# A fused attention and mixer kernel: six token tiles transposed by DMA, the first queries in column parts, and a second queue for loads

## The chip, the cores and the metric

The kernel runs on one core of one Trainium2 chip. The metric is the device time of one execution in microseconds (us), lower is better; three executions of the kernel before gave 1246.11, 1246.24 and 1246.83 us. A core has a matrix engine (TensorE, PE in the profile, with its weight loads shown as PEld), a vector engine (VectorE, DVE), a scalar engine (ScalarE, ACT), GpSimd (POOL) and a sync engine (SyncE, SP) that here only issues transfers. Transfers run on 16 DMA engines; SP and ACT each have a queue that feeds them (SPq and ACTq in the profile).

## The reference

The input `A_x` has 2048 tokens of width 512. It is normalised, and the result feeds two branches whose outputs are multiplied:

```python
xn = _layernorm(x)
# A: 32 heads of width 128, 2048 cached keys and values
q = (xn @ wq).reshape(B, Sq, H, Dh).transpose(0, 2, 1, 3)
p = _softmax(einsum("bhqd,bhkd->bhqk", q, k_cache) * (Dh ** -0.5))
s = einsum("bhqk,bhkd->bhqd", p, v_cache).transpose(0, 2, 1, 3).reshape(B, Sq, H * Dh) @ wo
# B: a mixer and an MLP on xn
h = _gelu(_layernorm(xn) @ w1)
hs = (the four column quarters of h, moved by +1, -1, +2, -2 tokens) @ w2
x1 = xn + hs
g = _silu(x1 + _gelu(_layernorm(x1) @ w3) @ w4)
return x + s * g
```

All arrays are bf16. The attention is by far the largest part.

## The kernel before, in words

A token tile is 128 tokens; there are 16 of them, t = 0 to 15. Every engine runs its own instructions in the order in which the program wrote them (`pin` keeps it), and waits between engines go by semaphores. DMAs take eight semaphores in turn, so each one also waits until the DMA issued eight before it has landed.

The program has a start of some 47 us, which this case is about, then the MLP, and then a long loop over 128 units (a head and 512 queries each) in which TensorE computes scores, ScalarE their exponentials, VectorE the sums, and TensorE the products with the values.

The start runs like this. `load_x` brings a token tile; tiles 0 to 7 are loaded first, tiles 1 and 3 and half of `w1` on ACT's queue and the rest on SP's. Behind them on SP come the four slices of `wq` for heads 0 to 3 (`load_w`), `w2`, and tiles 8 to 15. Eleven matmuls on zeros keep TensorE busy until the first tile is there.

`ln1(t, tr)` is the first normalisation: on VectorE the statistics of tile t + 1, then the normalised tile t into `xall`; the reciprocal root between them is on GpSimd. As the statistics of the next tile stand ahead of the normalisation, a late load of tile t + 1 holds tile t too, and everything behind it on VectorE. Then `tr` transposes the tile into `xnT`, which holds the tokens as columns. `tr_pe` does this with four 128-column matmuls against the identity into the PSUM pool `psO` and a ScalarE copy; `tr_dma` does it with one transposing DMA on SP, which needs neither.

`m1_tile` multiplies one transposed tile with `w1` (16 matmuls of 128 columns), `gelu_tile` applies the activation on ScalarE and writes `hT`; for tokens from 512 on, `m1(c0, 512)` does this for four tiles at once, with 16 matmuls of 512 columns. `m2(t)` multiplies four shifted pieces of `hT` with `w2` (four matmuls of 512 columns), and `x1(t)` adds the result to `xall` on VectorE, which frees the PSUM buffer of `m2(t)`. `q_mm` and `q_copy` make the queries of one unit: four matmuls of 512 columns into one of the two buffers `xa` and `xm` of the pool `psX`, and a copy to SBUF on ScalarE. `q_ahead` does both for a unit ahead of the loop and alternates between the two buffers.

Their order in the program before: tiles 0 to 3 are each transposed by TensorE, with `m1_tile` of tiles 0 to 3 between and behind them; for tiles 4 to 7 (`tr_q`) the queries of units 0 to 3 are made, each ahead of the TensorE transposition of one tile; then `m2` of tiles 0 and 1, `ln1` of tiles 8 to 11 with DMA transpositions, `m1(512, 512)`, `x1` of tiles 0 and 1, the queries of units 4 to 7, `m2` of tiles 2 and 3, `ln1` of tiles 12 to 15 with DMA transpositions, the loads of a further slice of `wq` and of `w3` on SP, `m1(1024, 512)`, and so on.

Of the kernel before, what the change touches and what calls it, by code (L numbers as in the profile page):

```python
# [10 lines left out]
FP32 = mybir.dt.float32  # L11
BF16 = mybir.dt.bfloat16
# [5 lines left out]
def kernel(  # L18
# [15 lines left out]
    nc = tc.nc  # L34
    P = nc.NUM_PARTITIONS

    x2d = A_x.flatten_outer_dims()
    out2d = out.flatten_outer_dims()
    Sq, D = x2d.shape
# [6 lines left out]
    DC = D // P  # L46
# [4 lines left out]
    HG = 4  # L51
# [10 lines left out]
    pin = tc.keep_in_program_order  # L62

    def pool(name, bufs=1, space=None, **kw):
        if space is not None:
            kw["space"] = space
        return tc.tile_pool(name=name, bufs=bufs, **kw)
# [3 lines left out]
    xnT = const.tile([P, DC, Sq], BF16, name="xnT")  # L71
# [19 lines left out]
    psO = ent(pool("psO", 2, PSUM))  # L91
    psX = ent(pool("psX", 1, PSUM))
    mid = ExitStack()
    psS = mid.enter_context(pool("psS", 2, PSUM, reuse_waits="tile"))
# [4 lines left out]
    pL = left.enter_context(pool("pL", reuse_waits="tile"))  # L99
# [4 lines left out]
    w2_v = B_w2.rearrange("(dc p) j -> p dc j", p=P)  # L104
    w3_v = B_w3.rearrange("(dc p) f -> p dc f", p=P)

    def mm(out, lhsT, rhs, start, stop):
        pin(nc.tensor.matmul(out=out, lhsT=lhsT, rhs=rhs, start=start, stop=stop))  # L108
# [7 lines left out]
        out=ident[:], in0=diag[:], scalar1=0.0, scalar2=None, op0=ALU.is_equal))  # L116

    units = [(g, qt, hh) for g in range(NG) for qt in range(QT) for hh in range(HG)]
# [5 lines left out]
    kTs, vBs, wqs, wos, oTs, st = {}, {}, {}, {}, {}, {}  # L124
# [30 lines left out]
    def load_w(h, eng=nc.sync):  # L155
        wqs[h] = wqp.tile([P, DC, Dh], BF16, name="wq_h")
        pin(eng.dma_start(out=wqs[h][:], in_=wq_v[:, :, h * Dh:(h + 1) * Dh]))

    vX = {}
    xin = {}  # L160

    def load_x(t, eng):
        xin[t] = tokp.tile([P, D], BF16, tag="ta", bufs=10, name="xin")
        pin(eng.dma_start(out=xin[t][:], in_=xsrc[t]))

    w1_sb = pL.tile([P, DC, D], BF16, name="w1_sb")
    w2_sb = pL.tile([P, DC, D], BF16, name="w2_sb")
# [22 lines left out]
    def ln1_stats(t):  # L192
        stats(xin[t][:], mv1, rs1, t)

    def ln1_norm(t):
        norm_to(xall[:, t, :], xin.pop(t)[:], mv1, rs1, t)

    def tr_pe(t):
        tp = psO.tile([P, DC, P], FP32, tag="ps_o", name="ps_o")
        for dc in range(DC):  # L200
            mm(tp[:, dc, :], xall[:, t, dc * P:(dc + 1) * P], ident[:], True, True)
        pin(nc.scalar.activation(out=xnT[:, :, t * P:(t + 1) * P], in_=tp[:], func=ACT.Identity))  # L202
# [17 lines left out]
    def m2(t, pl=psO, tag="ps_o"):  # L220
        ps = pl.tile([P, D], FP32, tag=tag, name="ps_o")
        for jc in range(DC):
            c0 = BASE_J[jc] + t * P - SHIFT[jc]
            mm(ps[:], hT[:, jc, c0:c0 + P], w2_sb[:, jc, :], jc == 0, jc == DC - 1)
        return ps
# [41 lines left out]
    def q_mm(u, dcs, tag="xa"):  # L267
        g, qt, hh = units[u]
        if dcs[0] == 0:
            st[u] = dict(psq=psX.tile([P, 512], FP32, tag=tag, name="ps_q"))  # L270
        for dc in dcs:
            mm(st[u]["psq"][:], wqs[g * HG + hh][:, dc, :],
               xnT[:, dc, qt * 512:(qt + 1) * 512], dc == 0, dc == DC - 1)

    def q_copy(u, eng=None):
        qT = qtp.tile([P, 512], BF16, name="qT")
        if eng is None:
            pin(nc.vector.tensor_copy(out=qT[:], in_=st[u].pop("psq")[:]))  # L278
        else:
            pin(nc.scalar.activation(out=qT[:], in_=st[u].pop("psq")[:], func=ACT.Identity))  # L280
        st[u]["qT"] = qT
# [227 lines left out]
    for t, eng in enumerate([nc.sync, nc.scalar, nc.sync]):  # L509
        load_x(t, eng)  # L510
    pin(nc.scalar.dma_start(out=w1_sb[:, 2:4, :], in_=w1_v[:, 2:4, :]))
    pin(nc.sync.dma_start(out=w1_sb[:, 0:2, :], in_=w1_v[:, 0:2, :]))
    load_x(3, nc.scalar)
    pin(nc.scalar.activation(out=junk[:], in_=ones_t[:], func=ACT.Gelu_apprx_tanh))
    for t in range(4, 8):
        load_x(t, nc.sync)
    for h in range(HG):
        load_w(h)
    pin(nc.sync.dma_start(out=w2_sb[:], in_=w2_v))
    wps = psX.tile([P, 512], FP32, tag="xm", name="ps_warm")  # L520

    def warm_mm(n):
# [9 lines left out]
    def ln1(t, tr):  # L532
        if t + 1 < NT:
            ln1_stats(t + 1)
        ln1_norm(t)
        tr(t)

    def m1_tile(t, pl, tag):
        ps = pl.tile([P, DC, P], FP32, tag=tag, name="ps_m1")
        for jc in range(DC):  # L540
            for dc in range(DC):
                mm(ps[:, jc, :], w1_sb[:, dc, jc * P:(jc + 1) * P],
                   xnT[:, dc, t * P:(t + 1) * P], dc == 0, dc == DC - 1)
        return ps

    def gelu_tile(t, ps):
        for jp in range(DC // 2):
            b = BASE_J[2 * jp] + t * P
            pin(nc.scalar.activation(
                out=hT[:, 2 * jp:2 * jp + 2, b:b + P], in_=ps[:, 2 * jp:2 * jp + 2, :],  # L550
                func=ACT.Gelu_apprx_tanh))
# [2 lines left out]
    ln1(0, tr_pe)  # L554
    warm_mm(1)
    ln1(1, tr_pe)
    pm = [m1_tile(0, psX, "xa")]
    ln1(2, tr_pe)
    gelu_tile(0, pm[0])
    pm.append(m1_tile(1, psX, "xm"))  # L560
    ln1(3, tr_pe)
    gelu_tile(1, pm[1])
    for t in (2, 3):
        gelu_tile(t, m1_tile(t, psS, "ps_s"))

    made = []

    def q_ahead(u):
        q_mm(u, range(DC), ("xa", "xm")[len(made) % 2])
        q_copy(u, nc.scalar)  # L570
        made.append(u)

    def tr_q(t):
        q_ahead(t - 4)
        tr_pe(t)

    for t in range(8, 16):
        load_x(t, nc.sync)
    for t in range(4, 8):
        ln1(t, tr_q)  # L580
    pend = [(t, m2(t)) for t in range(2)]
    for t in range(8, 12):
        ln1(t, tr_dma)
    m1(512, 512)
# [1 line left out]
        x1(t, ps)  # L586
    for u in range(HG, 2 * HG):
        q_ahead(u)
    pend = [(t, m2(t)) for t in range(2, 4)]
    for t in range(12, 16):  # L590
        ln1(t, tr_dma)
    wqs[H - 1] = pL.tile([P, DC, Dh], BF16, name="wq_e")
# [131 lines left out]
    for n in range(UB * SPU):  # L724
        u, p = divmod(n, SPU)
# [52 lines left out]
    t0 = 4 * (QT - 1)  # L778
# [144 lines left out]
```

## Time and profile before

| what | value |
|---|---|
| median of three executions | 1246.24 us |
| the profiled execution: its time | 1246.23 us |
| its span, first to last instruction | 1244.5 us |
| TensorE busy | 1231.6 us, 99% of the span |
| ScalarE busy | 1106.5 us, 89% |
| VectorE busy | 1008.4 us, 81% |
| first matmul on a token tile | at 5.87 us |
| first matmul of `m1(512, 512)` | at 17.68 us |
| first matmul of `m1(1024, 512)` | at 26.35 us |

Times in the profile count from the first instruction. The profiled execution's time is 1.7 us more than its span; it stands 0.01 us from the median, so it can be read as a typical one. A matmul's recorded duration (219 ns for 128 columns, 379 ns for 512) is longer than the distance to the next one, because matmuls overlap; the work is counted by the distance between starts, or by the pieces in the chain of work that ended last, which is told on from one instruction to the next.

### The profile page before, as it was taken

The page shows a single profiled execution, that of the slowest core. Times are in us where ns is not written, and L with a number is a line of the kernel's source. Part 1 is how long each engine was busy: PE and PEld are TensorE (multiplying, and loading weights), DVE is VectorE, ACT ScalarE, POOL GpSimd, SP SyncE. Part 2 cuts the span into 40 slices and gives each one's busy share as a digit, 9 for nine tenths or more (in the row PEclk, how much of TensorE's full clock was granted, in tenths as well). Part 3 has the DMA queues.
Part 4 walks back from the last instruction along what each step waited for, and adds up shares of the span by engine and source line. Part 5 has one row for each costly group of instructions (what it writes and reads, how often), then busy time and mean ns, then how long its engine had stood idle before and what let it go on. Part 6 is the DMA issues. An engine that isn't in the chain of part 4 may idle for free.

```text
span 1244.5 us, 16193 instructions
## 1 busy us (share of the span) xinstructions
PE 1231.6 (99%) x5757; PEld 606.7 (49%) x5873; DVE 1008.4 (81%) x1458; ACT 1106.5 (89%) x1112; POOL 27.4 (2%) x77
## 2 busy tenths in 40 slices
PE   9999999999999999999999999999999999999998
PEld 4444444444444444444444444444444444444445
DVE  7712778888888888888888888888888988999996
ACT  5344999999999999999999999999999999999996
POOL 5300000000000000000000000000000000000000
PEclk9999999999999999999999999999999999999999
DMA  6661123453345525553354424644345425553332
GB/s 179 149 135 35 26 44 64 102 103 81 63 80 109 101 48 85 84 117 77 56 102 86 106 55 69 104 101 72 72 86 113 101 59 90 98 111 62 79 77 65
DMA packets 241810, 107.15 MB, mean 86 GB/s; under 512 B 192704, under 2 KB 225472, under 8 KB 241728
## 3 DMA queue, kind: packets, MB, share of 16 engines
q1 hardware_dynamic: 241024, 105.51, 42.9%
q8 instruction: 46, 0.75, 0.3%
q10 hardware_dynamic: 704, 0.59, 0.1%
q14 instruction: 36, 0.29, 0.1%
HBM read 67.50 MB, written 2.36 MB: 56 GB/s over the span
## 4 chain that ended last, share of the span: by engine, by line
PE 98%; issue 1%; DVE 0%; ACT 0%; DMA 0%; POOL 0%; DVEq 0%
PE ps_s L108 41%; PE ps_o L108 38%; PE ps_q L108 8%; PE ps_wo L108 8%; PE ps_m L108 2%; PE ps_oh L108 0%; DMA xin<-in_A_x_dram 0%; ACT qT L280 0%; ACT xnT L202 0%; PE ps_w L108 0%; DVE tm L791 0%; DVE bn L183 0%; DVE y L808 0%; DVE xall L188 0%; DVE y L800 0%
## 5 line engine op out<-in xcount | busy, mean ns | idle before, releaser
L294 ACT ACTIVATE pT<-ps_s 128x1024 bf16<-128x1024 f32 x1016 | 1036.6, 1023 | 60.8 <-PE ps_s L108 7.7
L108 PE MATMUL ps_s<-qT,kT 128*128 128x512 bf16 (+1 forms) x2061 | 608.5, 377 | 5.1
L108 PE MATMUL ps_o<-pT,vb 128*128 128x512 bf16 x1979 | 589.0, 379 | 0.3
L305 DVE TENSOR_TENSOR acc<-acc,pT 128x2048 bf16<-128x2048 bf16 x254 | 307.5, 1211 | 104.5 <-ACT pT L294 104.2
L108 PEld LDWEIGHTS <-kT 128*128 128x128 bf16 x2064 | 234.0, 113 | 217.9
L108 PEld LDWEIGHTS <-vb 128*128 128x128 bf16 x1984 | 193.9, 98 | 216.7
L300 DVE TENSOR_TENSOR acc<-pT 128x2048 bf16<-128x2048 bf16 x127 | 155.2, 1222 | 39.3 <-ACT pT L294 39.1
L108 PE MATMUL ps_q<-xnT,wq_h 128*128 128x512 bf16 x459 | 168.5, 379 | 0.1
L108 PE MATMUL ps_wo<-wo_h,oT 128*128 128x512 bf16 x449 | 168.5, 379 | 0.0
L309 DVE TENSOR_TENSOR acc<-acc 128x1024 bf16<-128x1024 bf16 x127 | 87.9, 692 | 4.3
L366 DVE TENSOR_TENSOR oT<-ps_o,rb 128x512 bf16<-128x512 f32 x127 | 86.5, 681 | 1.3 <-DMA rb<-dr 0.8
L108 PEld LDWEIGHTS <-oT 128*128 128x128 bf16 x513 | 57.6, 113 | 58.5 <-ACT oT L490 0.3
L346 DVE TENSOR_REDUCE sm<-tT 128x4 f32<-128x512 bf16 x124 | 83.7, 675 | 0.3 <-DMA tT<-acc 0.3
L278 DVE CAST qT<-ps_q 128x512 bf16<-128x512 f32 x116 | 79.2, 683 | 0.0
L108 PEld LDWEIGHTS <-wq_h 128*128 128x128 bf16 x508 | 49.5, 98 | 59.1 <-issue 0.3
L430 DVE TENSOR_TENSOR sacc<-ps_wo,sacc 128x512 f32<-128x512 f32 x96 | 65.6, 683 | 0.0
L315 DVE TENSOR_TENSOR acc<-acc 128x512 bf16<-128x512 bf16 x126 | 53.6, 426 | 4.3
L245 ACT ACTIVATE h2T<-ps_s 128x1024 bf16<-128x1024 f32 x28 | 28.6, 1023 | 26.1 <-PE ps_s L108 25.4
L108 PE MATMUL ps_s<-xn2T,w_sb 128*128 128x512 bf16 x220 | 48.6, 379 | 0.2
L108 PEld LDWEIGHTS <-w_sb 128*128 128x128 bf16 x336 | 30.3, 98 | 32.1
L108 PEld LDWEIGHTS <-h2T 128*128 128x128 bf16 x224 | 21.9, 98 | 26.2
L108 PE MATMUL ps_m<-w_sb,h2T 128*128 128x512 bf16 x110 | 33.9, 379 | 0.2
(71 smaller groups left out, 329.1 us busy)
## 6 DMA issues: line engine op xcount, KB each, us to landing
rb<-dr SPq DMA_DIRECT2D x127, 256.0 KB, 4.1
vb<-in_A_v_cache_dram SPq DMA_DIRECT2D x62, 256.0 KB, 3.3
wq_h<-in_A_wq_dram SPq DMA_DIRECT2D x32, 128.0 KB, 3.5
wo_h<-in_A_wo_dram SPq DMA_DIRECT2D x32, 128.0 KB, 3.3
w_sb<-in_B_w_dram SPq DMA_DIRECT2D x8, 256.0 KB, 5.1
kT<-in_A_k_cache_dram SPq DMA_TRANSPOSE x128, 3.4
xl<-in_A_x_dram SPq DMA_DIRECT2D x16, 128.0 KB, 3.0
dr<-rc SPq DMA_DIRECT2D x127, 2.0 KB, 1.4
```

The lines of the kernel that those rows point to most:

```text
L108: pin(nc.tensor.matmul(out=out, lhsT=lhsT, rhs=rhs, start=start, stop=stop))
L245: pin(nc.scalar.activation(out=h2[c, f][:], in_=ps[:], func=ACT.Gelu_apprx_tanh))
L278: pin(nc.vector.tensor_copy(out=qT[:], in_=st[u].pop("psq")[:]))
L294: pin(nc.scalar.activation(out=s["pT"][-1][:, jj:jj + 2, :], in_=sps[:], func=ACT.Exp, scale=SCALE))
L300: pin(nc.vector.tensor_tensor(out=s["acc"][:], in0=s["pT"][0][:], in1=s["pT"][1][:], op=ALU.add))
L305: pin(nc.vector.tensor_tensor(out=a[:], in0=a[:], in1=st[u]["pT"][i][:], op=ALU.add))
L309: pin(nc.vector.tensor_tensor(out=a[:, 0:2, :], in0=a[:, 0:2, :], in1=a[:, 2:4, :], op=ALU.add))
L315: pin(nc.vector.tensor_tensor(out=a[:, 0, :], in0=a[:, 0, :], in1=a[:, 1, :], op=ALU.add))
L346: pin(nc.vector.tensor_reduce(out=sm[:], in_=s["tT"][:], axis=mybir.AxisListType.X, op=ALU.add))
L366: pin(nc.vector.tensor_tensor(out=to, in0=o, in1=rb, op=ALU.mult))
L430: pin(nc.vector.tensor_tensor(out=sa, in0=ps[:], in1=sa, op=ALU.add))
```

## The change

Four things are done together, all in the start.

1. `tr_dma` takes the place of `tr_pe` for tiles 2 to 7. Tiles 0 and 1 stay on TensorE. Twenty-four identity matmuls and six ScalarE copies are gone, six transposing DMAs come on SP's queue.
2. The queries of units 0 to 3 are made in column parts (`q_cols`), each part as soon as its tiles are transposed: tokens 0 to 255 for all four units after `m1` of tile 1, the rest between and behind `m1` of tiles 2 and 3. Units 0 and 1 use the buffers `xa` and `xm`, units 2 and 3 the two of `psO`. This makes 40 matmuls of 256 or 128 columns of the 16 of 512.
3. `w2` and tiles 8 to 15, these as four pairs of 256 KB (`load_pair`), are issued on ACT's queue, among ScalarE's activations: the pair of tiles 8 and 9 behind the activation of tile 0, `w2` and the pair of 10 and 11 behind that of tile 1, the pairs of 12 and 13 and of 14 and 15 behind the four query copies. SP issues nine DMAs fewer there.
4. `m2` of tile 2 moves ahead of `m1(512, 512)`, into the buffer `xa`; `x1` of tile 2 moves with it, behind `ln1` of tile 11 on VectorE. `xa` is also the buffer of the queries of unit 4.

```diff
+    def load_pair(t, eng):
+        pair = pL.tile([P, 2, D], BF16, tag="xp", bufs=4, name="xin")
+        pin(eng.dma_start(out=pair[:], in_=x2d[t * P:(t + 2) * P, :].rearrange("(i p) d -> p i d", p=P)))
+        xin[t], xin[t + 1] = pair[:, 0, :], pair[:, 1, :]
...
-    pin(nc.sync.dma_start(out=w2_sb[:], in_=w2_v))
...
     ln1(0, tr_pe)
     warm_mm(1)
     ln1(1, tr_pe)
-    pm = [m1_tile(0, psX, "xa")]
-    ln1(2, tr_pe)
-    gelu_tile(0, pm[0])
-    pm.append(m1_tile(1, psX, "xm"))
-    ln1(3, tr_pe)
-    gelu_tile(1, pm[1])
-    for t in (2, 3):
-        gelu_tile(t, m1_tile(t, psS, "ps_s"))
-
-    made = []
+    def m1_gelu(t, pl, tag):
+        gelu_tile(t, m1_tile(t, pl, tag))
+
+    def q_cols(u, t0, t1):
+        g, qt, hh = units[u]
+        if t0 == 0:
+            pl, tag = ((psX, "xa"), (psX, "xm"), (psO, "ps_o"), (psO, "ps_o"))[u]
+            st[u] = dict(psq=pl.tile([P, 512], FP32, tag=tag, name="ps_q"))
+        for dc in range(DC):
+            mm(st[u]["psq"][:, t0 * P:t1 * P], wqs[g * HG + hh][:, dc, :],
+               xnT[:, dc, t0 * P:t1 * P], dc == 0, dc == DC - 1)
+        if t1 == 4:
+            q_copy(u, nc.scalar)
+
+    m1_gelu(0, psS, "ps_s")
+    load_pair(8, nc.scalar)
+    ln1(2, tr_dma)
+    m1_gelu(1, psS, "ps_s")
+    pin(nc.scalar.dma_start(out=w2_sb[:], in_=w2_v))
+    load_pair(10, nc.scalar)
+    ln1(3, tr_dma)
+    for u in range(HG):
+        q_cols(u, 0, 2)
+    m1_gelu(2, psS, "ps_s")
+    ln1(4, tr_dma)
+    for u in (0, 1):
+        q_cols(u, 2, 3)
+    m1_gelu(3, psS, "ps_s")
+    ln1(5, tr_dma)
+    for u in (2, 3):
+        q_cols(u, 2, 4)
+    for u in (0, 1):
+        q_cols(u, 3, 4)
+    for t in (12, 14):
+        load_pair(t, nc.scalar)
+    for t in (6, 7):
+        ln1(t, tr_dma)
+    made = list(range(HG))
...
-    def tr_q(t):
-        q_ahead(t - 4)
-        tr_pe(t)
-
-    for t in range(8, 16):
-        load_x(t, nc.sync)
-    for t in range(4, 8):
-        ln1(t, tr_q)
-    pend = [(t, m2(t)) for t in range(2)]
+    pend = [(t, m2(t, *((psX, "xa") if t == 2 else (psO, "ps_o")))) for t in range(3)]
     for t in range(8, 12):
         ln1(t, tr_dma)
     m1(512, 512)
     for t, ps in pend:
         x1(t, ps)
     for u in range(HG, 2 * HG):
         q_ahead(u)
-    pend = [(t, m2(t)) for t in range(2, 4)]
+    pend = [(3, m2(3))]
     for t in range(12, 16):
         ln1(t, tr_dma)
```

## The prediction

> **What bounds the kernel now.** First the page: busy shares and the chain that ended last.
>
> ```profile
> PE 1231.6 (99%) x5757; PEld 606.7 (49%) x5873; DVE 1008.4 (81%) x1458; ACT 1106.5 (89%) x1112; POOL 27.4 (2%) x77
> ...
> PEclk9999999999999999999999999999999999999999
> ...
> PE 98%; issue 1%; DVE 0%; ACT 0%; DMA 0%; POOL 0%; DVEq 0%
> ```
>
> TensorE is the bound from end to end, at full granted clock. A microsecond taken from or added to its queue in the start moves the end by as much, unless a later wait takes it up, and the chain shows hardly any. Other engines count only where TensorE waits for them. So next, busy time by stretch: to the first m1 of 512 columns (17.68), and to the next (26.35).
>
> ```profile
> 7.20:17.68 10.48, 10.37 (x115) 7.31 (x114) 10.17 (x28) 8.45 (x19) 8.12 (x18) 1.00 0.75 203
> 17.68:26.35 8.67, 8.62 (x41) 3.91 (x40) 6.62 (x16) 4.33 (x6) 4.17 (x9) 1.00 0.48 95
> ```
>
> After the length of the stretch come PE, PEld, DVE, ACT and POOL. TensorE is full in both; VectorE has 10.17 of 10.48 us in the first, so lateness there isn't made good before 17.68. Third, the chain in order of time, whose pieces give the prices of matmuls.
>
> ```profile
> 7.38 0.89 PE ps_m L108 x16
> 8.28 0.28 PE ps_o L108 x4
> ...
> 9.45 0.29 PE ps_o L108 x4
> ...
> 24.79 1.73 PE ps_o L108 x8
> 26.51 3.45 PE ps_s L108 x16
> ```
>
> A matmul of 128 columns costs 0.056 us (0.89/16), one of 512 0.216 (3.45/16), so one of 256 some 0.108 by halving. The four identity matmuls should take 0.22 and took 0.28 and 0.29: 0.06 and 0.07 of waiting for VectorE. Last the timeline and the groups by tile for SP and VectorE.
>
> ```profile
> 8.18 3.87 SPq L164 DMA_DIRECT2D xin<-in_A_x_dram  x8
> ...
> 17.43 0.69 DVE L183 BATCH_NORM_STATS2 bn<-xin 128x6 f32<-128x512 bf16 x1
> ...
> 18.28 0.41 DVE L188 TENSOR_SCALAR xall<-xin,mv,rs 128x512 bf16<-128x512 bf16 x1
> 18.61 1.28 DVE L228 TENSOR_TENSOR xall<-ps_o,xall 128x512 bf16<-128x512 f32 x2
> ```
> ```profile
> L205 SPq DMA_TRANSPOSE xnT<-xall x8: 1195/1216/1320, 15.2 to 24.9; - x8
> ...
> DMA to landing us min/median/max: 2.4/2.5/2.7
> ```
>
> One transposing DMA holds SP 1.22 us; the single rows stand 1.31 apart where nothing is waited for (16.61, 17.90, 19.21). It lands 2.5 us after its start. The rows of 17.43 to 18.61 are the statistics of tile 12, the normalisation of tile 11, and the first two x1: the order that decides below.
>
> **The change part by part.** I follow TensorE from 7.22, the first m1 matmul, which nothing in the change moves.
>
> *Removed.* 24 identity matmuls x 0.056 = 1.34 us of TensorE. The two waits on VectorE, 0.13, go with them, and the wait of m2 of tile 1 for the copy of tile 7 on ScalarE (one start distance of 0.44 instead of 0.216 at 16.4): 0.23. Six copies of 0.59 leave ScalarE, which isn't the bound (8.45 of 10.48).
>
> *Query parts.* The 40 matmuls cover the same columns as the 16. The only overhead I can read is 0.056 against a quarter of 0.216: 0.002 each, nothing. TensorE: m1 of tiles 0 and 1 to 9.00; sixteen matmuls of 256 columns, 1.73, to 10.73. The wq slices land at 8.78, 9.33, 9.71 and 10.08, each before its use at 9.00, 9.43, 9.87 and 10.30.
>
> *Transpositions on SP.* VectorE ends the normalisation of tiles 2 to 7 at 8.10, 9.28, 10.45, 11.63, 12.81 and 13.98. SP ends the wq issues at 7.57, and w2 and the eight loads behind them are gone from it. So tile 2 starts at 8.13 and, as 1.31 is more than VectorE's 1.18, SP sets the pace: tile 3 at 9.44, tile 7 at 14.68. With 2.5 to landing: tile 2 at 10.6, tile 3 at 11.9, tile 7 at 17.2. TensorE wants tile 2 at 10.73 and, 0.89 and eight small matmuls (0.45) later, tile 3 at 12.07: no wait. It then runs m1 of tile 3, 0.86 and 0.45 of query parts, to 14.28, and three m2 (2.59) to 16.87. m1 of tokens 512 to 1023 needs tile 7, so it begins at 17.2, 0.33 later than it could. Before it began at 17.68 with one m2 (0.86) less behind it: 0.48 + 0.86 = 1.34 gained here.
> How the transpositions go beside loads isn't shown: before, the last load landed at 16.12, before the first transposition's data would. From below: 2.4, the least row. From above: loads stretched from 2.7 to 4.9 when many were in flight, so 1.8 times, 4.5. I take 2.5 for tile 7, because the loads around it are few (below); 4.5 is a rival.
>
> *Loads on ACT's queue.* Five issues of some 0.46 (the row of half of w1), 2.3 us of ScalarE against 3.5 freed: nothing on the path by themselves, but each goes only after the activations ahead of it. Whether at the start or the end of the last one isn't shown; that is 0.6 at most.
> The pair 8/9 goes after the activation of tile 0, about 8.6; 256 KB took 3.7 (w1's ACT half, five other loads near it), so 12.3, against its use by the statistics of tile 8 at 12.73. w2 goes at about 9.5 and took 4.0 on SP: 13.5, against m2 at 14.28. The pair 10/11 follows at 10.1, 14.0 or so, against 15.1. With the worst loads (4.9 for an x tile, 5.8 for w3) these would be up to 0.8 late; hidden in the forecast, in the range otherwise.
> The pair 12/13 stands behind the four query copies. ScalarE does the activation of tile 3 from about 13.2 and four copies of 0.59, starting 0.5 apart, from 13.85: the last runs from 15.35 to 15.95. I put the issue at 15.6. Landing: 2.6 from below (an unhurried 128 KB, w4's least 2.3, and 0.36, the distance of landings of x tiles, for the second half), 3.7 from above, 3.1 in the middle: 18.7, with ends 17.9 and 19.7. Before, tile 12 had landed by 14 to 15 and VectorE took it at 17.43.
>
> *The new wait.* Behind the statistics of tile 12 VectorE has the normalisation of tile 11 and then x1 of tiles 0, 1 and, new, 2. From 17.43 to the end of the second x1 is 2.46; a third adds 0.68: 3.14. x1 of tile 2 ends at 18.7 + 3.14 = 21.85, and only then is the buffer xa free for the queries of unit 4. TensorE is there at 17.2 + 3.45 = 20.65. It waits 1.2 us (ends: 0.4 and 2.2). Queued behind it on TensorE: queries of units 4 to 7 and m2 of tile 3; they end at 21.85 + 3.45 + 0.86 = 26.16, against 26.35 before.
> Later nothing: tiles 8 to 11 must be transposed by 26.2, and tile 11, normalised at 19.9, lands near 23. Tiles 12 to 15 are normalised some 1.3 us later than before, which puts the last wq slice, landing at 28.6 before and used at 32.4, still in time, and w3 (36.2) ten us before its use at 47.3.
>
> *Sum.* 26.35 - 26.16 = 0.19 gained; I keep 0.15 for semaphores. The profiled execution took 1246.23 us, span 1244.5 and 1.7 around it, 0.01 under the median; so 1246.23 - 0.15 = **1246.1 us**. As a balance: 1.70 removed, 0.33 and 1.2 of new waits.
>
> **The rivals.**
>
> *The loads on ACT run early.* If the pair 12/13 need not wait for the copies but only for its semaphore (the transposition of tile 4, issued at 10.75, landed at 13.3), it lands at 16.4 and VectorE is on time: x1 of tile 2 ends at 17.43 + 3.14 = 20.57, before TensorE's 20.65. The whole 1.34 stays: 1244.9 us. For it: in no row before does a DMA on ACT follow an activation, so nothing denies it. Against: the rows of every queue are in program order. [...]
>
> *Slower: the pair 12/13 lands late.* One mechanism, at the x1 of tile 2. If it takes 4.9, as the slowest x tile did, it lands at 20.5, x1 ends at 23.64, and the stretch at 27.95: 1.6 lost, 1247.8 us. It turns to a loss where the pair lands after 18.9, 3.3 after the issue. For it: it shares the engines with the transpositions of tiles 7 to 9 and the last pair. Against: these are few; w4's loads of 128 KB took 2.3 to 3.0 in a quiet stretch.
>
> *Transpositions slowed by loads.* If tile 7 takes 4.5, m1 begins at 19.2 and ends at 22.65; the wait for x1 is then hidden, since 21.85 has passed. The stretch ends at 26.96: 0.6 lost, 1246.8 us. For it: DMA share 0.75 in the stretch. Against: by 15 us the loads of this stretch have landed. [...] Before, tiles 8 to 15 showed 2.5 with no load beside them.
>
> *Several of these, w2 among them, at once*: 2 to 4 us lost, about 1249.
>
> **How the numbers follow.** Forecast 0.45; early loads 0.22; late pair 0.18; slowed transpositions 0.10; several 0.05. The forecast's own range, from the pair landing between 17.9 and 19.3, is 1245.3 to 1246.7. Leaving out 0.1 at each side: 1244.7 to 1248.0. About 0.2% (2.5 us) is what a measurement of this kernel tells from no change. More than 1.70 can't be gained, as that is all that goes, so faster 0.02 for what I don't see; slower 0.07, from several at once and the far end of the late pair; same 0.91.
>
> **What would show it.** Right: tiles 2 to 7 in SPq from 8.1, 1.3 apart; first 512-column m1 near 17.2; a wait of VectorE for the DMA of a pair near 17.4; TensorE idle about 1 us before the queries of unit 4; m1 of 1024 to 1535 at about 26.2, and from there on the same distances as before. Wrong: ACT's loads ahead of activations that precede them; idle TensorE between 10.7 and 12.1, or 17.2 and 19; any difference that arises after 27 us.

## The result and the profile after

The changed kernel takes 1250.61 us (median of 7 runs, 1248.76 to 1251.25) against 1246.13 (7 runs, 1245.88 to 1246.83): 1.0033 times the time before, 95% interval 1.0023 to 1.0043. It is slower by 0.33%, beyond the 0.2% that the prediction named as its limit. 1246.1 was forecast, with a range to 1248.0.

The execution that was profiled took 1249.88 us, with a span of 1248.0. From its page: the busy shares and the chain that ended last, by engine.

```profile
PE 1236.6 (99%) x5873; PEld 606.9 (49%) x5873; DVE 1008.3 (81%) x1458; ACT 1103.8 (88%) x1106; POOL 27.3 (2%) x77
...
PEclk9999999999999999999999999999999999999999
...
PE 98%; DMA 1%; DVE 1%; ACT 0%; issue 0%; POOL 0%; DVEq 0%
```

TensorE is still the bound, and the chain now holds one per cent of DMA where it had 0%. The busy time by stretch shows where. The first stretch goes from the first m1 matmul to m1 of tokens 512 to 1023, the second to m1 of tokens 1024 to 1535; behind the length stand PE, PEld, DVE, ACT and POOL, the granted clock, the DMA share and GB/s.

```profile
7.00:21.12 14.12, 10.07 (x120) 7.97 (x117) 10.02 (x27) 5.20 (x13) 8.61 (x19) 1.00 1.02 191
21.12:29.55 8.43, 7.93 (x38) 3.51 (x37) 6.47 (x16) 4.44 (x6) 3.54 (x8) 1.00 0.45 105
```

TensorE was busy for all but 0.11 of 10.48 us in the first stretch before. Now it idles for 4.05 of 14.12, and for 0.50 of 8.43 in the second. m1 of 1024 starts at 29.55 instead of 26.35, 3.20 later. From there to m1 of 1536 both kernels take 10.39, and the last output matmuls start 3.39 later (1239.52 against 1236.13): the loss is made in the first 30 us. The waits between 7 and 30 us (engine, tile, what it waited for: us in total, times, the longest) say for what:

```profile
DVE bn L188 <- DMA xin<-in_A_x_dram: 4.8, 2, 3.9
PE ps_m L108 <- DMA xnT<-xall: 4.0, 2, 2.9
...
PE ps_q L108 <- DVE xall L233: 0.5, 1, 0.5
```

Two waits of m1 for a transposed tile, and one of the queries of unit 4 for x1 of tile 2. Taken by the starts of the matmuls on either side, less one matmul, they are 1.35 us (for tile 2), 3.02 (tile 3) and 0.66. The view by tile shows SP's issues and the landings:

```profile
L210 SPq DMA_TRANSPOSE xnT<-xall x6: 1217/1228/1312, 7.9 to 14.6; - x6
...
DMA to landing us min/median/max: 3.8/4.8/6.8
```

SP starts them when it was expected to, at 7.91, 9.33, 10.64, 11.97, 13.29 and 14.61. But they land 3.84, 6.78, 5.68, 4.87, 4.01 and 4.79 us later, where 2.4 to 2.7 were the rows before. Tile 3 lands at 16.11. The chain in order of time (start, us, what) follows it from there:

```profile
9.33 6.78 DMA xnT<-xall
16.11 0.14 issue
16.24 1.07 PE ps_m L108 x16
17.31 0.02 issue
17.33 0.66 ACT hT L553 x2
17.99 0.67 ACT qT L285 x2
18.66 3.49 DMA xin<-in_A_x_dram
...
23.00 0.38 DVE xall L193
23.38 1.81 DVE xall L233 x3
25.19 0.04 issue
25.23 3.61 PE ps_q L108 x16
```

One late tile makes the whole path. m1 of tile 3 starts late, so ScalarE's activation of it and the query copies are late, so the load of the pair 12/13, which stands behind them on ScalarE's queue, is issued at 18.66. Its statistics on VectorE wait, the normalisation of tile 11 and the three x1 follow, and with the last of them `xa` comes free.

What travels beside the transpositions are the loads of ScalarE's queue: the pair 8/9 from 8.10 to 11.18, `w2` from 8.99 to 14.65, the pair 10/11 from 9.66 to 15.87. The DMA packets that the trace shows in half a microsecond, SP's queue (256 B each) against ScalarE's (1 KB each):

```
from us   13.0  13.5  14.0  14.5 | 15.5  16.0  16.5
SP         128   109   126   114 |  499   507   511
ScalarE     91   109   115    98 |    0     0     0
```

From 13.0 to 15.0 the packets of the two queues come out about one to one, 477 to 413. From 11.0 to 13.0, while the transposition of tile 3 was in flight, SP's fared worse: 232 came out beside 348 of ScalarE's. Once ScalarE's are done, SP's go about four times as fast. From 9.00 to 14.50 the core moves 221 GB/s, where it moved 288 before.

The clock adds a part that this profiled execution doesn't show. The mean granted clock over each of the seven runs was 1.000 in those of 1248.76 and 1249.88 us, and 0.998 in the five of 1250.22 to 1251.25; the difference of the means is 1.4 us. A second trace (the second experiment) shows what can lie behind 0.998.

### The profile page after: what moved, and what is told of

Read it like the earlier page. It is cut to its first block, busy times and chain, and to the rows that moved or that the text cites. A ratio compares the mean times of both kernels' runs of the same rounds, so it can differ in the third digit from the quotient of the medians.

```text
span 1248.0 us, 16306 instructions
## 1 busy us (share of the span) xinstructions
PE 1236.6 (99%) x5873; PEld 606.9 (49%) x5873; DVE 1008.3 (81%) x1458; ACT 1103.8 (88%) x1106; POOL 27.3 (2%) x77
## 4 chain that ended last, share of the span: by engine, by line
PE 98%; DMA 1%; DVE 1%; ACT 0%; issue 0%; POOL 0%; DVEq 0%
PE ps_s L108 40%; PE ps_o L108 38%; PE ps_wo L108 9%; PE ps_q L108 9%; PE ps_m L108 2%; DMA xnT<-xall 1%; DMA xin<-in_A_x_dram 0%; PE ps_oh L108 0%; DVE bn L188 0%; DVE xall L193 0%; DVE xall L233 0%; PE ps_w L108 0%; DVE tm L815 0%; DVE mv L189 0%; DVE y L832 0%
## 5 line engine op out<-in xcount | busy, mean ns | idle before, releaser
L299 ACT ACTIVATE pT<-ps_s 128x1024 bf16<-128x1024 f32 x1016 | 1037.1, 1023 | 60.6 <-PE ps_s L108 7.0
L108 PE MATMUL ps_q<-xnT,wq_h 128*128 128x512 bf16 (+2 forms) x532 | 186.3, 369 | 0.5 <-DVE xall L233 0.5
L108 PE MATMUL ps_wo<-wo_h,oT 128*128 128x512 bf16 x496 | 186.2, 379 | 0.0
L250 ACT ACTIVATE h2T<-ps_s 128x1024 bf16<-128x1024 f32 x28 | 28.6, 1023 | 26.1 <-PE ps_s L108 26.1
```

The source lines that it names most:

```text
L250: pin(nc.scalar.activation(out=h2[c, f][:], in_=ps[:], func=ACT.Gelu_apprx_tanh))
L299: pin(nc.scalar.activation(out=s["pT"][-1][:, jj:jj + 2, :], in_=sps[:], func=ACT.Exp, scale=SCALE))
```

## The experiments

Theory 1: the transpositions of tiles 2 and 3 are late because the loads on ScalarE's queue go beside them, about packet for packet by the counts from 13.0 to 15.0 (477 to 413). Theory 2: transposing DMAs take this long here in any case, through what SP's queue itself has in flight and what VectorE and the matmuls do. Theory 3, on the time: part of the loss is TensorE's clock, halved after the waits. The kernel before took 1246.34, 1246.27 and 1246.26 us (medians) beside them.

**The loads taken away.** Pairs and `w2` are constants that VectorE writes, not loads; one buffer serves as all four pairs.

```diff
+            pin(nc.vector.memset(one["p"][:], 0.5))
...
+    pin(nc.vector.memset(w2_sb[:], 0.01))
...
-    load_pair(8, nc.scalar)
...
-    pin(nc.scalar.dma_start(out=w2_sb[:], in_=w2_v))
-    load_pair(10, nc.scalar)
...
-    for t in (12, 14):
-        load_pair(t, nc.scalar)
```

> Leaves out the loads of w2 and of tiles 8 to 15 (w2 and one pair tile are set to constants on VectorE before the first tile lands, so the values of tiles 8 to 15 and of the mixer are not the reference's); the rest is the changed kernel. Theory 1, the loads slow the transpositions: each of tiles 2 to 7 lands 2.4 to 2.6 us after its issue, TensorE waits neither at 10.5 nor at 13.2 nor before the queries of unit 4, m1 of tokens 512 on starts near 17.0, time 1244.6 to 1245.1. Rival 2, the transpositions are slow by themselves when six are issued in a row behind wq: landings stay 4 to 6 us after the issue, TensorE still waits some 2 to 3 us for tile 3, time 1248 to 1249.

Measured: 1247.46 us (1247.29 to 1247.62), ratio 1.0009 (1.0000 to 1.0018). The transpositions and the wait of TensorE, by tile and in the list of waits:

```profile
L214 SPq DMA_TRANSPOSE xnT<-xall x5: 1208/1220/2257, 9.0 to 14.4; - x5
...
DMA to landing us min/median/max: 2.4/2.5/4.0
```
```profile
PE ps_s L108 <- DMA xnT<-xall: 1.3, 1, 1.3
```

Tiles 2, 3 and 4 land 2.52, 2.41 and 2.43 us after their issue, and nothing waits for them or at unit 4. That the loads make these three late is shown. The time is 2.4 above the 1245.1 that theory 1 allowed. The constants delay the start by some 0.9 us (the transposition of tile 1 starts at 7.89, where the kernel before had 6.98), so I estimate 1246.6 without them: even with no load beside the transpositions no gain is left. The other 1.45 is a wait of m1 of 512 for tile 7 (by the starts of the matmuls, less one matmul): tiles 5 and 6 still took 4.02 and 3.50, and tile 7 was issued behind them only at 16.73. A transfer of 16 KB on the queue that the trace calls instruction falls at 14.08, beside these two.

**The changed kernel once more**, for a second trace.

> The changed kernel once more, for a second trace of it. If the executions near 1250.6 to 1251.3 differ from the profiled 1249.9 by the landing of tile 3, this trace shows it at 16.5 to 18 where the time is above 1250.2, with all matmuls at full granted clock from 5 us on; if they differ by the clock, a stretch of lower granted clock stands behind the idle 3 us.

Measured: 1250.82 us, clock 0.998. Tile 3 landed 6.70 us after its issue. Three stretches of this trace, in the columns of the first windows:

```profile
13.60:16.00 2.40, 0.22 (x4) 0.04 (x1) 1.67 (x5) 0.47 (x2) 1.88 (x5) 1.00 1.22 233
16.00:19.43 3.43, 2.90 (x22) 2.57 (x23) 2.32 (x6) 0.81 (x3) 1.81 (x5) 0.50 1.00 147
19.43:22.70 3.27, 3.27 (x24) 1.82 (x22) 0.00 (x0) 2.01 (x4) 0.00 (x0) 1.00 0.67 164
```

Late in a wait of 2.9 us for tile 3 (13.60 to 16.52) the clock is halved, from 16.01 to 19.43. m1 of 512 starts at 22.71, 1.6 later than in the first trace. The wait at unit 4 shrinks to 0.3, since TensorE itself is later, and m1 of 1024 starts at 30.76, 1.2 later. The first trace had a wait as long and kept its clock; the last section sets the two side by side.

**The loads on SP's queue**, at the same places of the program.

```diff
-    load_pair(8, nc.scalar)
+    load_pair(8, nc.sync)
...
-    pin(nc.scalar.dma_start(out=w2_sb[:], in_=w2_v))
-    load_pair(10, nc.scalar)
+    pin(nc.sync.dma_start(out=w2_sb[:], in_=w2_v))
+    load_pair(10, nc.sync)
...
-        load_pair(t, nc.scalar)
+        load_pair(t, nc.sync)
```

> The changed kernel with w2 and the four pairs on SP's queue, in the same places of the program. Theory 1, two queues take turns packet by packet, so that a 256 B packet of a transposition goes for every 1 KB packet of a load: in one queue this ends, tile 3 lands only behind w2 and the pair 10/11, near 13.7 instead of 16.1, TensorE's wait for it is 1 to 1.8 us instead of 3.0, the pair 12/13 is in time and the wait before unit 4 is gone; 1246.5 to 1247.5. Rival 2, only the bytes on the 16 engines count, in whichever queue: tile 3 lands near 16 again and the time stays at 1249 or above.

Measured: 1249.29 us (1248.82 to 1249.75), ratio 1.0024 (1.0015 to 1.0033). Landing by tile, and the waits for transposed tiles:

```profile
DMA to landing us min/median/max: 2.5/3.4/4.4
```
```profile
PE ps_m L108 <- DMA xnT<-xall: 2.5, 2, 2.1
...
PE ps_s L108 <- DMA xnT<-xall: 0.8, 1, 0.8
```

Tile 3 now lands 4.11 us after its issue instead of 6.78, but is issued 1.5 later (10.86), as SP has the loads to issue as well: it lands at 14.96, between the two forecasts. The time lies above what theory 1 gave and within what the rival gave, so this run doesn't separate them by the time. `w2` takes 4.04 instead of 5.66, and the loads alone run at 346 GB/s between 11.5 and 13.5. So with two queues both sides took longer, but one queue didn't take the loads out of the way: in this trace what was issued ahead went first. From 12.0 to 13.5 the queue sends 558 packets of loads and 4 of transpositions, with tile 3's issued since 10.86.

**`w2` early**: its load goes at the head of ScalarE's queue, ahead of the activations.

```diff
     load_x(3, nc.scalar)
+    pin(nc.scalar.dma_start(out=w2_sb[:], in_=w2_v))
...
-    pin(nc.scalar.dma_start(out=w2_sb[:], in_=w2_v))
     load_pair(10, nc.scalar)
```

> The changed kernel with w2's load moved to the head of ACT's queue, behind the load of tile 3, so that it is gone before the first transposing DMA. Theory 1, the 1 KB packets queued on ACT at the time of the transpositions set how late those land: only 256 KB go beside tiles 2 and 3 each, tile 3 lands 3 to 5 us after its issue instead of 6.8, the wait of TensorE for it falls from 3.0 to under 1.5, and the time to 1246.8 to 1248.6, though the wq slices land 1 to 1.5 us later. Rival 2, transpositions beside any load are slow, however little is queued: tile 3 stays at 6 to 7 us after its issue and the time at 1249.5 or above.

Measured: 1249.36 us (1247.89 to 1251.74), ratio 1.0024 (1.0015 to 1.0034). The median misses what theory 1 gave by 0.8 us. The waits of TensorE in the trace, whose execution of 1251.74 is the slowest of the ten:

```profile
PE ps_s L108 <- DMA xnT<-xall: 2.3, 1, 2.3
...
PE ps_q L108 <- DMA wq_h<-in_A_wq_dram: 1.6, 1, 1.6
...
PE ps_m L108 <- DMA xnT<-xall: 0.8, 1, 0.8
```

Tile 3 lands after 4.00 us, as theory 1 expected with 512 KB less beside it. But `w2` now travels beside the `wq` slices, the last of which land at 11.52 and 11.89, so the queries leave a gap of 1.84 between starts, and tile 7 takes 6.07 (with an instruction transfer at 15.87) and costs 2.6 between starts, after which the clock is 0.5 from 23.45 to 26.87. The load was moved from one wanted transfer onto two others.

**The pairs 12/13 and 14/15 on SP's queue.**

```diff
     for t in (12, 14):
-        load_pair(t, nc.scalar)
+        load_pair(t, nc.sync)
```

> The changed kernel with only the pairs 12/13 and 14/15 on SP's queue, behind the transposition of tile 5. Theory, the wait before the queries of unit 4 (0.66 us in the profile) is the late pair 12/13 through x1 of tile 2: the pair lands before VectorE asks for it, the wait goes, tile 3 stays late, time 0.5 to 0.9 below the changed kernel, 1249.5 to 1250.2. Rival, that wait comes from VectorE itself, late by the pair 10/11: it stays, and the time is 1250.3 to 1251.

Measured: 1250.88 us (1249.46 to 1251.99), ratio 1.0036 (1.0023 to 1.0049). The wait at unit 4 is gone from the trace, since the pair 12/13 goes from 13.59 to 17.85. m1 of 1024 starts at 29.21, 0.33 earlier than in the first trace of the change, so the last link of the chain was read rightly. The time doesn't show it: the median lies where the rival put it, the runs spread over 2.5 us, and four of the five have a mean clock of 0.996 to 0.999.

**Zero matmuls in the gap**, first 12 and then 3 of 512 columns ahead of m1 of tile 3, to keep the clock up.

```diff
+    wps = psS.tile([P, 2, 512], FP32, tag="ps_s", name="ps_fill")
+    for _ in range(12):
+        mm(wps[:, 0, :], warm[:, 0:P], warm[:], True, True)
     m1_gelu(3, psS, "ps_s")
```

> The changed kernel with twelve matmuls of 512 columns on zeros (2.6 us) on TensorE ahead of m1 of tile 3, where it waited 3.0 us in the profile. Theory, the idle stretch of 3 us lowers the granted clock in the executions where it is a little longer, and that is the distance between the profiled 1249.9 and the median 1250.6: with the stretch filled the clock is 1.000 in all executions, the spread is under 0.6 us, time 1248.8 to 1249.9. Rival, the distance has another cause: the clock stays at 0.998 in most executions and the time is 1250.2 to 1251.3, or more where the fill comes late.

> The changed kernel with three matmuls of 512 columns on zeros (0.65 us) ahead of m1 of tile 3, too few to move the fetch of instructions into the wait. Theory, the clock of TensorE is halved for 3.4 us after a wait of about 2.9 to 3.0 us, as the second trace of the changed kernel showed, and this makes the difference between its executions near 1249.9 and near 1250.8: with the wait cut to 2.3 us the granted clock is 0.999 or 1.000 in nearly all executions and the median is 1249.2 to 1250.2. Rival, the difference lies in when tile 3 lands: the spread and the median stay at 1250.3 to 1251.3.

Measured: 1251.12 us (1250.76 to 1252.74; 1.0040, 1.0028 to 1.0053) with 12, and 1250.23 (1248.86 to 1251.21; 1.0030, 1.0020 to 1.0041) with 3. Neither is a cure. With 12, four of five runs have a clock of 0.999 or 1.000, but tile 3 landed later still (8.01 us after its issue, at 17.70), so TensorE waited all the same; the instruction transfer lies at 15.80 in that trace. With 3, the trace has two waits of 1.3 us (10.15 to 11.50 and 11.84 to 13.10) and half clock from 13.60 to 17.02. Its median lies at the edge of the theory's range. Its eight runs give an estimate of what the drop costs: four with a mean clock of 0.999 or 1.000 take 1248.86 to 1250.26 (mean 1249.57), four with 0.998 take 1250.21 to 1251.21 (mean 1250.76). That is 1.2 us, if 0.998 marks the runs with a drop in the start. It need not: without the loads, three runs with 0.998 took 1247.44 to 1247.62, no longer than the others.

**Tiles 2 to 7 back on TensorE**, the rest of the change kept.

```diff
+    def tr_ps(t):
+        tp = psS.tile([P, DC, P], FP32, tag="ps_s", name="ps_t")
+        for dc in range(DC):
+            mm(tp[:, dc, :], xall[:, t, dc * P:(dc + 1) * P], ident[:], True, True)
+        pin(nc.scalar.activation(out=xnT[:, :, t * P:(t + 1) * P], in_=tp[:], func=ACT.Identity))
...
-    ln1(2, tr_dma)
+    ln1(2, tr_ps)
...
```

> The changed kernel with tiles 2 to 7 transposed by TensorE again (into the buffers of psS, with ScalarE copies); query parts, loads on ACT's queue and the early m2 of tile 2 stay. Theory, the transposing DMAs alone carry the loss: without them no wait at tiles 2 and 3, w2 lands 4 to 4.5 us after its issue instead of 5.7, time 1246.0 to 1247.5. Rival, the loads on ACT's queue or the query parts cost by themselves: 1248.5 or above.

Measured: 1247.17 us (1246.99 to 1247.66), ratio 1.0008 (0.9999 to 1.0016), as expected. m1 of 512 starts at 19.26, and the longest wait of TensorE before it is for an activation:

```profile
PE ps_m L108 <- ACT hT L553: 0.5, 1, 0.5
```

So 3.4 of the 4.5 us between the medians hang on transposing by DMA, though the 24 identity matmuls (1.34 us) are back. Of the 0.9 that is left, most goes with waits of 0.63 and 0.24 between starts, for the activation that frees a buffer of `psS`; `tr_ps` takes its own from there too. The loads gain too: `w2` takes 4.06 instead of 5.66, the pair 10/11 4.45 instead of 6.21.

**Only tiles 2 and 3 back on TensorE**: `tr_ps` for these two, tiles 4 to 7 by DMA, the loads on ScalarE's queue.

> The changed kernel with only tiles 2 and 3 back on TensorE (into psS, with ScalarE copies); tiles 4 to 7 by DMA, loads on ACT's queue, query parts and the early m2 stay. Theory, the loss is that the two tiles which TensorE wants at once, 2 and 3, go through a 4 to 7 us transposition, and that everything behind them in ScalarE's order, the load of tiles 12 and 13 too, is late with them: without that no wait at 10.5 and 13.2, the pair 12/13 goes at 15.5 to 16.5 instead of 18.7 to 20.3, m1 of tokens 512 on starts at 17.2 to 19, time 1246.2 to 1248.0. Rival, the waits only move to tiles 4 to 7, whose transpositions now meet the same loads: m1 of tokens 512 on starts at 20 or later, time 1249 or above.

Measured: 1247.82 us (1247.51 to 1248.45), ratio 1.0012 (1.0004 to 1.0021). By tile, and the wait that stays:

```profile
L210 SPq DMA_TRANSPOSE xnT<-xall x4: 1218/1267/1943, 10.5 to 14.6; - x4
...
DMA to landing us min/median/max: 4.0/5.2/6.6
```
```profile
PE ps_q L108 <- DVE xall L233: 1.5, 1, 1.5
```

Tiles 4 to 7 are as slow as in the change, but TensorE wants them later: m1 of 512 starts at 18.71 with 0.8 between starts ahead of it (tile 7 landed at 18.62). With TensorE on time, the load of the pair 12/13 (17.56 to 20.76, where an issue at 15.5 to 16.5 was expected) is what is late, and the queries of unit 4 wait 1.7 between starts, less one matmul, for x1 of tile 2. What holds the load here isn't ScalarE, whose last copy starts at 16.32, but the semaphore: the DMA issued eight before is the transposition of tile 5, as the chain shows.

```profile
11.96 5.58 DMA xnT<-xall
17.54 0.02 issue
17.56 3.20 DMA xin<-in_A_x_dram
```

So here a transposition of 5.58 us also held back a load on the other queue. The clock stays at 0.999 or above in all runs, and they spread over 0.9 us.

**One queue, wanted late**: the kernel before, with tiles 4, 5 and 6 by DMA and the loads of tiles 12 to 15 issued behind them on SP. Nothing of the change's other parts.

```diff
-        tr_pe(t)
+        (tr_dma if t < 7 else tr_pe)(t)
...
-    for t in range(8, 16):
+    for t in range(8, 12):
         load_x(t, nc.sync)
     for t in range(4, 8):
         ln1(t, tr_q)
+        if t == 6:
+            for i in range(12, 16):
+                load_x(i, nc.sync)
```

> The kernel before with tiles 4, 5 and 6 transposed by DMA on SP instead of TensorE, and the loads of tiles 12 to 15 moved behind them on SP; tile 7 stays on TensorE, all loads on one queue. Theory, DMA transposition pays where the tiles are wanted late and the loads ahead are in the same queue: 12 identity matmuls (0.67 us) go and tile 6 lands before m1 of tokens 512 on asks for it near 17: 1245.5 to 1246.0. Rival, tile 6 is late here too, behind the loads or the fetch of instructions near 13.6: 1246.5 or above.

Measured: 1245.93 us (1245.77 to 1246.27), ratio 0.9998 (0.9989 to 1.0006): the lowest median of all, 0.34 below the kernel before beside it, and no difference that the interval allows one to claim. By tile, and by stretch as above:

```profile
L205 SPq DMA_TRANSPOSE xnT<-xall x3: 1217/1307/1879, 10.5 to 13.9; - x3
...
DMA to landing us min/median/max: 2.5/3.4/4.4
```
```profile
7.00:17.02 10.02, 9.93 (x104) 6.82 (x105) 9.64 (x25) 6.99 (x16) 7.65 (x18) 1.00 0.98 202
17.02:25.69 8.67, 8.67 (x41) 3.92 (x40) 7.40 (x19) 4.33 (x6) 4.73 (x11) 1.00 0.61 137
```

The first of them takes 4.43 us here as well, behind loads in its own queue and with an instruction transfer at 12.30, but it lands at 14.93, and m1 of 512, which needs it, starts at 17.02. TensorE is full in both stretches, and m1 of 1024 starts at 25.69, 0.65 before its time in the kernel before.

## Why the prediction was wrong, point by point

- *Removed, 1.70 us: right.* From the first m1 (7.22 before, 7.00 after) to m1 of 1024, before took 19.13 and after 22.55, 3.42 more. The three waits are 5.03; less 1.70 that makes 3.33, so what was to go did go.
- *Query parts, nothing: right.* TensorE's excess is in the three waits but for 0.09, so 40 parts cost no more than 16 matmuls. The balance tests this and the 1.70 together, not each alone.
- *SP's pace: right.* 8.13 and 1.31 apart were forecast; 7.91 and 1.31 to 1.42 measured.
- *Transpositions on SP, "no wait": the step that failed.* "With 2.5 to landing" was taken for tiles 2 and 3 from rows of tiles 8 to 15, which ran with no load beside them, and the step put `w2` and two pairs, 1 MB in all, on the engines at just that time. The upper end of 4.5 was applied to tile 7 alone ("I take 2.5 for tile 7, because the loads around it are few"), though the step behind it had the loads landing between 12.3 and 14.0, when tiles 2 and 3 are wanted. Measured: 3.84 and 6.78, so 1.35 and 3.02 of waiting for a term that stood at nothing, and 6.78 lies beyond the upper end too. Idle TensorE between 10.7 and 12.1, which the prediction named as a sign of being wrong, is there (10.42 to 11.88). Without the loads the landing is 2.41 to 2.52; the loads are the cause, shown for tiles 2 to 4. How the engines share themselves out between two queues, no run shows beyond the counts: from 13.0 to 15.0 about one to one, 477 to 413, so that SP's packets of 256 B beside ScalarE's of 1 KB were 22% of the bytes; from 11.0 to 13.0 fewer, 232 to 348, for a reason that no run shows.
- *The 0.33 ahead of m1 of 512: gone.* Tile 7 landed at 19.41 (17.2 forecast), but m1 of 512 stood at 21.12 by then for the sake of tile 3.
- *Loads on ScalarE, issue at the start or the end of the last activation: it is neither, but earlier.* The pair 8/9 stands behind both activations of tile 0; it goes 9 ns after the start of the first (8.091, 8.100) and ahead of the second (8.371). The pair 12/13 passes two copies, as this order of time of ScalarE and its DMA queue in the changed kernel shows (start, us, engine, operation):

```profile
17.88 1.10 ACT L285 ACTIVATE qT<-ps_q 128x512 bf16<-128x512 f32 x2
18.66 0.37 ACTq L168 DMA_DIRECT2D xin<-in_A_x_dram  x1
18.83 0.63 ACT L285 ACTIVATE qT<-ps_q 128x512 bf16<-128x512 f32 x1
```

  So the rival of early loads had half the mechanism: the issue at 18.66 didn't wait for the copies to end, and the last two start behind it at 18.83 and 19.30, but the copies ahead of it, late by tile 3, held it. Its time wasn't 15.6 but 18.66, through tile 3. The loads themselves took longer too: `w2` landed at 14.65 and the pair 10/11 at 15.87, where 13.5 and 14.0 were forecast.
- *The new wait, 1.2 us: right in mechanism, 0.66 in the change.* Pair and TensorE were both late by the same tile. With TensorE on time it was 1.7, but that this is near 1.2 is luck: there the pair waited for its semaphore, behind the transposition of tile 5, and not for the copies. The prediction held the issue of the pair and the landing of tile 3 for separate things; they are one chain, so the rivals' prices didn't add up one beside the other but ran one behind the other.
- *The rival "transpositions slowed by loads"* had the right cause at the wrong tile: on tile 7 it cost 0.6 and gave 1246.8; on tile 3, whose wait was put at nothing, it cost 3.02.
- *TensorE's clock* had no term. Waits of 1.3 to 3.0 us stood in it for the first time. One trace of the change shows the drop that can follow; the five runs of seven with a mean clock of 0.998 took 1.4 us longer than the other two, so up to 1.4 of the 4.5 us can be put down to it.
- *Nothing after 27 us: right in substance*, with the mark moved to 30: 3.20 there, 3.39 at the end.

## What to carry to other kernels

A second DMA queue didn't keep the two kinds of transfer apart here: beside loads in packets of 1 KB on the other queue, a transposing DMA in packets of 256 B came out 3.8 to 6.8 us after its issue instead of 2.5, and `w2` took 5.66 us instead of the 4.06 with tiles 2 to 7 on TensorE. Price a transposition by rows with the same loads beside it, and move to DMA only those tiles that the bound engine wants after they have landed at that price. Tiles 4 to 6 were wanted 6.5, 5.1 and 3.1 us after their issue and landed after 4.4, 3.4 and 2.5, without a wait; tiles 2 and 3 were wanted too soon. When several steps hang on one late transfer, follow the delay through every queue and every shared semaphore in order, as the price of one wait decides whether the next exists.

## What was not expected of the hardware

- **The clock and short waits.** The granted clock fell to 0.5 for 3.4 us late in a wait of 2.9 us (second trace of the change, 16.01 to 19.43), after one of 2.6 (`w2` early, 23.45 to 26.87), and after two of 1.3 with work between (3 fills, 13.60 to 17.02); it did not fall with one of 3.0 (first trace of the change). So the length of the wait alone didn't decide. In the 3.4 us just ahead of those three drops TensorE was idle, by its busy time, for 2.19, 2.15 and 2.07 us. In the trace of the kernel before, a clock of 1.00 is recorded from 4.913 to the drop behind the last matmuls, for 1239.038 us; in the first trace of the change from 4.596, for 1242.451 us. The two lengths are 3.413 us apart, 363 and 364 times that, and the three drops are 3.42 long by their times. From these numbers I estimate that the clock changes only at steps of 3.413 us, counted from where that record starts. By this estimate a step ends at 14.84 in the first trace of the change and cuts the wait of 3.0 us (13.17 to 16.24) in two: TensorE is idle for 1.91 us of the step from 11.42 and for 1.41 of the one from 14.84, and neither had a drop behind it; in the second trace a step from 12.60 to 16.01 holds most of the wait. As the record starts at another time in each of these two traces, it would be luck whether such a wait costs a drop. How much idle time it takes, and where, no run shows.
- **The instruction queue.** The first transfer of 16 KB on the queue that the trace calls instruction, 0.93 us long before and 1.32 after, comes when TensorE has started 218 and 219 matmuls and weight loads: at 13.58 before, where no transposition is in flight, and at 17.23 after; it stands at 14.08, 16.78 and 15.80 in three other traces. Where there was no load at all, the two transpositions beside it landed 1.1 to 1.6 us later than the others (4.02 and 3.50 instead of 2.4). That it is the cause is read from where they coincide; no run moved this transfer alone.
